# The last head's second V pair in one load, and wo in loads of 24, 6, 1 and 1 rows

## The chip, the cores and the metric

The kernel runs on one core of a Trainium2 chip. The metric is device time in microseconds (us) for one execution; the value for the kernel before is the median of three runs. Beside the runs there is one profiled execution. Its trace covers a span from the first to the last instruction, which is a little shorter than the execution's time. A position such as 358.86 is a number of microseconds from the start of that span.

## The reference

One token passes through two branches, and a gate mixes them. Branch A is attention over a long cache with grouped heads; branch B is a small gated MLP.

```python
# A: x (1,1,1024), k_cache and v_cache (1,4,65536,128), wq (1024,4096), wo (4096,1024), all bf16
q = (x @ wq) as 32 heads of 128
k, v = each of the 4 cached heads repeated for 8 query heads
p = softmax((q . k) * 128 ** -0.5)
a = (p @ v, the 32 heads side by side) @ wo
# B: w_in (1024,3584), w_out (1792,1024)
z = gelu(x @ w_in); z1, z2 = halves of z; z2 = layernorm(z2)
b = (z1 * (w_sp * z2 + b_sp)) @ w_out
# mix
g = sigmoid(sum(x * gate_w))
out = g * a + (1 - g) * b
```

The K and V caches are 67 MB each, so nearly everything that the kernel moves is cache: 162 MB are read in all, and each byte is used once.

## The kernel before

**Tiles.** A cached head has 65,536 rows of 128 values. It is cut into four tiles, 4 MB each, numbered j = 0 to 3 (`NT` = 4). In a tile each of the 128 partitions holds 128 rows (32 KB). Tiles come in pairs from one stretch of 256 rows per partition, so a load of two tiles reads 64 KB of each partition in one piece. All loads go into one SBUF buffer, `kv`, of five slots of 32 KB per partition (`NKV` = 5). `load(src, shape, at)` (L177) issues one DMA from SP into the slots from `at` on, and `load_kv` (L189) loads n tiles of one head from tile j on and returns the views. Reads and writes of the same slots order each other: a load waits until the last reader of what was there is done.

**The stages.** First come w_in and wq, the small branch's first half and the queries (L197 to L384). Then for each cached head g: four times `k_tile` (L407), which transposes the tile on DVE and multiplies it with the queries on PE; `stats(g)` (L431), the maximum, the exponentials on ACT and their transposes on DVE; four times `v_tile` (L457), 32 matmuls on PE for each tile, with 64 columns of weights each and 512 streamed columns, that accumulate into `o_ps`; and `head_out(g)` (L472). The loop at L529 interleaves the K tiles of head g with the V tiles of head g - 1. The last head's V tiles follow after the loop (L549 to L551).

**`head_out(g)`** takes the diagonal blocks of `o_ps` on DVE (L474), sums them into `o_sb` (L478), sends that and the sums of the exponentials through two small PE matmuls into `om_ps` (L482, L484), and ends with five short DVE instructions, the last of which writes the normalised and gated head into `oa` (L496).

**The projection.** `wo_view` gives each partition its 32 rows of wo, 2 KB each. The loop at L559 loads them in the pieces of `WO_SPLIT`, from slot 3 on, so that the first piece needs slot 3 free, which the last head's second V tile used. After each load `project` (L511) multiplies its rows with `oa`: four matmuls a row, of 256 streamed columns each, in four column groups of PE that run side by side. All of it accumulates into `out_ps`, in which `uT @ w_out` of branch B already stands. ACT then casts `out_ps` (L566), and two small DMAs from the queues of ACT and SP store it (L569).

**Filler matmuls.** `keep_busy(n)` (L499) issues n matmuls of 128x128 weights and 512 streamed columns on PE, whose results nobody reads. They are the instructions with `busy_ps` in the profile. In the kernel before, six stand ahead of the last `head_out`, sixteen after it, and `WO_BUSY` gives how many follow each piece of wo: none after the 24 rows, two after the 4 rows, one after the 2 rows, none after the single rows.

**Order.** The block at L572 to L579 makes each engine keep the order of the program as written. PE therefore meets V tiles, fillers, `head_out`'s matmuls and projection exactly in the order of the code, and SP issues the loads in theirs. Repeated weight loads of one operand are dropped (`same_weights`).

Of the kernel before, what the change touches and what calls it, by code (L numbers as in the profile page):

```python
# [21 lines left out]
CC = CT // VC  # L22
ZN = 448
HN = 512
WO_SPLIT = (24, 4, 2, 1, 1)
WO_BUSY = {24: 0, 4: 2, 2: 1, 1: 0}


@with_exitstack
def kernel(  # L30
# [18 lines left out]
    _, G, S, DH = A_k_cache.shape  # L49
# [15 lines left out]
    assert S % (P * CT) == 0 and F == 2 * NB * ZN and ZN == B * FC and HD == NHB * NB * HN  # L65
    assert NHB * NB == 2 * G and CC * B == 2 * HN and sum(WO_SPLIT) == OC

# [12 lines left out]
    def same_weights(ins):  # L80
        held.add(ins.ins.name)
# [95 lines left out]
    def load(src, shape, at):  # L177
        n = 1
        for s in shape:
            n *= s  # L180
        v = kv[:, int(at * CT * P):int(at * CT * P) + n]
        if len(shape) == 2:
            v = v.rearrange("p (a b) -> p a b", b=shape[1])
        ins = nc.sync.dma_start(out=v, in_=src)  # L184
        if not first_load:
            first_load.append(ins.ins.name)
        return v

    def load_kv(src, g, j, at, n=1):  # L189
        h, i = divmod(j, 2)  # L190
        rows = src[0, g, 2 * h * CT * P:2 * (h + 1) * CT * P, :].rearrange(
            "(p c) d -> p (c d)", c=2 * CT)
        v = load(rows[:, i * CT * DH:(i + n) * CT * DH], (n * CT * DH,), at)
        return [v[:, i * CT * DH:(i + 1) * CT * DH] for i in range(n)]
# [166 lines left out]
    for k in range(NHB):  # L361
# [3 lines left out]
                                                                   j=B, e=2),  # L365
# [91 lines left out]
    def v_tile(g, j, vt):  # L457
        if j == 0:
            o_ps[g] = pso.tile([P, 2, VC * DH], FP32, name="o_ps")
        vx = vt.rearrange("p (v c d) -> p c v d", v=VC, d=DH)  # L460
        for u in range(CC // 2):
            hs = slice(u % 2 * P // 2, (u % 2 + 1) * P // 2)
            for e in range(2):
                ins = nc.tensor.matmul(  # L464
                    o_ps[g][hs, e, :],
                    lhsT=ptt[g, j][:, 2 * u:2 * u + 2, :].rearrange("p c x -> p (c x)"),
                    rhs=vx[:, 2 * u + e], start=(j == 0 and u < 2),
                    stop=(j == NT - 1 and u >= CC // 2 - 2), skip_group_check=True)
                if e > 0:
                    same_weights(ins)  # L470

    def head_out(g):  # L472
        gs = slice(g * B, (g + 1) * B)
        nc.vector.tensor_tensor(  # L474
            out=om8, in0=o_ps[g][:].rearrange("p e (v d) -> p (e v) d", d=DH),
            in1=own_8[:].unsqueeze(2).to_broadcast([P, 2 * VC, DH]), op=ALU.mult)
        o_sb = wk.tile([P, DH], FP32, name="o_sb")
        nc.vector.tensor_reduce(out=o_sb[:], in_=om8.rearrange("p x d -> p d x"), axis=AX.X,  # L478
                                op=ALU.add)
        om_ps = psm.tile([P, DH + NT], FP32, name="om_ps", tag="m")  # L480
        hs = hsel[:].rearrange("p h q -> p (h q)")
        nc.tensor.matmul(om_ps[gs, DH:], lhsT=hs, rhs=lss[g][:], start=True, stop=True,  # L482
                         skip_group_check=True)
        nc.tensor.matmul(om_ps[gs, :DH], lhsT=hs, rhs=o_sb[:], start=True, stop=True,  # L484
                         skip_group_check=True)
        rl = wk.tile([P, 2], FP32, name="rl")
        nc.vector.reduce_sum(out=rl[gs, 0:1], in_=om_ps[gs, DH:], axis=AX.X)
        nc.vector.reciprocal(out=rl[gs, 1:2], in_=rl[gs, 0:1])
        om = wk.tile([P, QD, OC], FP32, name="om")
        nc.vector.tensor_tensor(  # L490
            out=om[gs], in0=om_ps[gs, :DH].rearrange("p (q c) -> p q c", c=OC),
            in1=own_q[gs, :].unsqueeze(2).to_broadcast([B, QD, OC]), op=ALU.mult)
        osum = wk.tile([P, OC], FP32, name="osum")
        nc.vector.tensor_reduce(out=osum[gs, :], in_=om[gs].rearrange("p q c -> p c q"),
                                axis=AX.X, op=ALU.add)
        nc.vector.tensor_scalar(out=oa[gs, :], in0=osum[gs, :], scalar1=rl[gs, 1:2],  # L496
                                scalar2=gate[gs, :], op0=ALU.mult, op1=ALU.mult)

    def keep_busy(n):  # L499
        ps = pss.tile([P, 2 * HN], FP32, name="busy_ps", tag="s")  # L500
        w = wt[G % 2][:].rearrange("p v b t u h -> p (v b t u h)")
        for i in range(n):
            ins = nc.tensor.matmul(ps[:, :HN], lhsT=w[:, :P], rhs=w[:, :HN], start=True,  # L503
                                   stop=True, skip_group_check=True)
            if i > 0:
                same_weights(ins)
# [4 lines left out]
    def project(w, n, vec, c0, first=False, last=False):  # L511
        for c in range(n):
            for t in range(NB):
                nc.tensor.matmul(  # L514
                    out_ps[t * B:(t + 1) * B, :],
                    lhsT=vec[:, c0 + c:c0 + c + 1].to_broadcast([P, B]),
                    rhs=w[:, c, t * NO:(t + 1) * NO],
                    start=(first and c == 0), stop=(last and c == n - 1),
                    skip_group_check=True)
# [9 lines left out]
    for g in range(1, G):  # L529
# [16 lines left out]
            if h == 0 and g + 1 < G:  # L546
                build_w(g + 1)
        head_out(g - 1)
    for j, n, at in ((0, 2, 2), (2, 1, 1), (3, 1, 0)):  # L549
        for i, vt in enumerate(load_kv(A_v_cache, G - 1, j, at, n)):  # L550
            v_tile(G - 1, j + i, vt)  # L551
    keep_busy(6)
    head_out(G - 1)
    keep_busy(16)


    wo_view = A_wo.rearrange("(p c) n -> p c n", c=OC)
    c0 = 0
    for n in WO_SPLIT:  # L559
        t = load(wo_view[:, c0:c0 + n, :], (n, D), 3 + c0 * D / (CT * P))  # L560
        project(t, n, oa, c0, last=(c0 + n == OC))
        keep_busy(WO_BUSY[n])
        c0 += n
# [46 lines left out]
```

## Time and profile before

| | |
|---|---|
| median of 3 runs | 381.88 us (381.71 to 381.96) |
| the profiled execution's own time | 381.88 us |
| its span | 380.5 us |
| mean granted TensorE clock | 0.839 |
| PE busy | 226.4 us (60%) |
| DVE busy | 211.2 us (56%) |
| ACT busy | 39.6 us (10%) |
| read from HBM | 162.01 MB, 426 GB/s over the span |
| share of the SP queue's packets in 16 DMA engines' span | 98.8% |

The page of the profile has these parts. A table of 40 slices of equal length gives for each engine the busy share in tenths (9 is 90% or more); the row PEclk is the clock that PE was granted, in tenths of full speed, and the row DMA is the mean busy share of the core's 16 DMA engines. The chain of waits follows the work back from the last instruction to what released it; each line has a start, a length and what it was. A timeline line has a start, a length, the engine, the line of the kernel (L464 is line 464), the operation, what it writes and reads, shapes, a count, and in brackets how long the engine had been idle and what ended that. In windows, each line is a stretch with its length, PE's busy time with the number of matmuls, the mean granted clock, the DMA share and GB/s. A matmul's end in the trace is modelled[...], so the last one of a row of matmuls looks longer than the spacing between them.

### The profile page before, as it was taken

The numbers are of one execution on the slowest core, as the hardware profiler recorded it, in microseconds if no ns is written. First come the engines' busy times: TensorE is split into PE (matmuls) and PEld (weight loads), VectorE is DVE, ScalarE is ACT, GpSimd is POOL, SyncE is SP. The second block draws the span as 40 slices with busy tenths as digits, with TensorE's granted clock in tenths as the row PEclk, the third lists the DMA queues.
The fourth block names the chain that finished last, engine by engine and source line by source line (L and its number), as shares of the span: only waits on it lengthen the run. The fifth ranks groups of instructions, "written<-read, shape, count | busy, mean of one in ns | idle before, by whom it ended". The sixth has DMA issues, their size and how long they took to land.

```text
span 380.5 us, 2602 instructions
## 1 busy us (share of the span) xinstructions
PE 226.4 (60%) x1397; PEld 55.6 (15%) x800; DVE 211.2 (56%) x207; ACT 39.6 (10%) x55; POOL 4.4 (1%) x10
## 2 busy tenths in 40 slices
PE   0060605967655784794499139762993197739386
PEld 0010101211211210121022001110220011202113
DVE  4134217989374947867893058678940397650040
ACT  1001000111104310114011001140110010500000
POOL 4000000000000000000000000000000000000000
PEclk9995765999958796999599758995898599959789
DMA  9999999999999999999999999999999999999995
GB/s 386 476 420 413 401 442 441 441 472 410 407 422 441 441 443 434 434 434 441 441 429 441 434 441 420 422 413 442 434 434 429 427 434 442 436 410 434 431 432 224
DMA packets 3655, 162.17 MB, mean 426 GB/s; under 512 B 440, under 2 KB 444, under 8 KB 828
## 3 DMA queue, kind: packets, MB, share of 16 engines
q1 hardware_dynamic: 3604, 162.01, 98.8%
q8 instruction: 8, 0.13, 0.1%
q14 instruction: 3, 0.02, 0.0%
q10 hardware_dynamic: 40, 0.01, 0.0%
HBM read 162.01 MB, written 0.00 MB: 426 GB/s over the span
## 4 chain that ended last, share of the span: by engine, by line
DMA 71%; PE 17%; DVE 9%; issue 2%; SPq 0%; ACTq 0%; ACT 0%; DVEq 0%
DMA kv<-in_A_k_cache_dram 52%; PE s_ps L419 13%; DVE kv L412 8%; DMA kv<-in_A_wo_dram 7%; DMA kv<-in_A_v_cache_dram 7%; DMA wb<-in_B_b_sp_dram 5%; PE o_ps L464 2%; PE z_ps L296 1%; SPq L184 0%; DVE mx L402 0%; ACTq L198 0%; PE small_ps L271 0%; ACT out_sb L566 0%; PE out_ps L514 0%; ACTq L199 0%
## 5 line engine op out<-in xcount | busy, mean ns | idle before, releaser
L419 PE MATMUL s_ps<-kv,wt 128*128 128x512 bf16 x512 | 132.8, 414 | 81.4 <-DVE kv L412 81.3
L412 DVE STREAM_TRANSPOSE kv<-kv 128x2048 int32<-128x2048 int32 x64 | 142.4, 2280 | 69.7 <-DMA kv<-in_A_k_cache_dram 69.7
L464 PE MATMUL o_ps<-kv,pt 128*64 128x512 bf16 x512 | 63.6, 408 | 14.3 <-DMA kv<-in_A_v_cache_dram 14.3
L419 PEld LDWEIGHTS <-wt 128*128 128x128 bf16 x256 | 26.4, 103 | 189.2 <-issue 117.9
L428 ACT CAST sc<-s_ps 128x1024 bf16<-128x1024 f32 x16 | 16.2, 1013 | 250.7 <-PE s_ps L419 250.7
L464 PEld LDWEIGHTS <-pt 128*64 128x64 bf16 x256 | 16.9, 117 | 57.9 <-issue 48.6
L454 DVE STREAM_TRANSPOSE pt<-sc 128x1024 bf16<-128x1024 bf16 x16 | 18.6, 1217 | 6.8 <-ACT sc L451 6.8
L474 DVE TENSOR_TENSOR rowt<-o_ps,own 128x1024 f32<-128x1024 f32 x4 | 4.8, 1195 | 26.5 <-PE o_ps L464 26.5
L451 ACT ACTIVATE sc<-sc,nb 128x1024 bf16<-128x1024 bf16 x16 | 18.2, 1137 | 12.2 <-DVE nb L447 12.2
L484 PE MATMUL om_ps<-o_sb,hsel 128*32 128x128 f32 x8 | 2.3, 388 | 18.3 <-DVE o_sb L478 18.3
L402 DVE TENSOR_TENSOR mx<-mx,sc 128x1024 bf16<-128x1024 bf16 x8 | 5.5, 687 | 13.6 <-ACT sc L428 13.6
L296 PE MATMUL q_ps<-kv,xT 128*32 128x512 bf16 x64 | 5.7, 534 | 7.2 <-DMA kv<-in_A_wq_dram 7.2
L252 PE MATMUL xb_ps<-xg,spread 8*128 8x256 bf16 x1 | 0.4, 364 | 13.5 <-DMA xg<-in_gate_w_dram 13.5
L478 DVE TENSOR_REDUCE o_sb<-rowt 128x128 f32<-128x1024 f32 x4 | 7.5, 1872 | 0.1
L363 DVE TENSOR_TENSOR rowt<-q_ps,own_b 128x512 f32<-128x512 f32 x2 | 1.3, 686 | 10.8 <-PE q_ps L296 10.8
L503 PE MATMUL busy_ps<-wt 128*128 128x512 bf16 x25 | 6.1, 381 | 0.0
L296 PE MATMUL z_ps<-kv,xT 128*32 128x448 bf16 x64 | 6.1, 572 | 0.0
L566 ACT CAST out_sb<-out_ps 128x256 bf16<-128x256 f32 x1 | 0.4, 372 | 46.4 <-PE out_ps L514 46.4
L256 DVE TENSOR_TENSOR xm<-xb_ps,sel_i 128x128 f32<-128x128 f32 x2 | 0.5, 286 | 8.2 <-PE xb_ps L252 8.2
L514 PE MATMUL out_ps<-kv,oa 128*32 128x256 bf16 x128 | 4.2, 273 | 1.4 <-DMA kv<-in_A_wo_dram 1.4
L435 DVE TENSOR_REDUCE m<-mx 128x1 f32<-128x1024 bf16 x4 | 4.8, 1209 | 0.1
L296 PEld LDWEIGHTS <-xT 128*32 128x32 bf16 x64 | 2.6, 137 | 14.7 <-issue 14.6
(90 smaller groups left out, 61.2 us busy)
## 6 DMA issues: line engine op xcount, KB each, us to landing
kv<-in_A_v_cache_dram SPq DMA_DIRECT2D x2, 4096.0 KB, 22.8
kv<-in_B_w_in_dram SPq DMA_DIRECT2D x1, 7168.0 KB, 19.7
kv<-in_A_wo_dram SPq DMA_DIRECT2D x1, 6144.0 KB
kv<-in_B_w_out_dram SPq DMA_DIRECT2D x1, 3584.0 KB
kv<-in_A_wo_dram SPq DMA_DIRECT2D x1, 1024.0 KB, 26.8
kv<-in_A_wo_dram SPq DMA_DIRECT2D x1, 512.0 KB
kv<-in_A_wo_dram SPq DMA_DIRECT2D x2, 256.0 KB
kv<-in_A_k_cache_dram SPq DMA_DIRECT2D x8, 27.6
```

The lines of the kernel that those rows point to most:

```text
L296: ins = nc.tensor.matmul(ps[t * B:(t + 1) * B, k * HN:k * HN + n], lhsT=xT[:, i * KH + c:i * KH + c + 1].to_broadcast([P, B]), rhs=w[:, c, ...
L402: nc.vector.tensor_tensor(out=mx[:], in0=mxs[g][:], in1=sc[:], op=ALU.max)
L412: nc.vector.transpose(out=kb[:, v * n:(v + 1) * n], in_=kb[:, v * n:(v + 1) * n])
L419: ins = nc.tensor.matmul(s_ps[:, k * HN:(k + 1) * HN], lhsT=wt[g % 2][:, v, b].rearrange("p a v h -> p (a v h)"), rhs=kx[:, b // 2, b % 2, ...
L428: nc.scalar.copy(out=sct[g, j][:], in_=s_ps[:])
L435: nc.vector.reduce_max(out=m1[:], in_=mxs[g][:], axis=AX.X)
L451: nc.scalar.activation(out=sct[g, j][:], in_=sct[g, j][:], func=ACT.Exp, scale=SCALE, bias=nb[:, 0:1], accum_out=lss[g][:, j:j + 1])
L454: nc.vector.transpose(out=ptt[g, j][:].rearrange("p c x -> p (c x)"), in_=sct[g, j][:])
L464: ins = nc.tensor.matmul(o_ps[g][hs, e, :], lhsT=ptt[g, j][:, 2 * u:2 * u + 2, :].rearrange("p c x -> p (c x)"), rhs=vx[:, 2 * u + e], sta ...
L474: nc.vector.tensor_tensor(out=om8, in0=o_ps[g][:].rearrange("p e (v d) -> p (e v) d", d=DH), in1=own_8[:].unsqueeze(2).to_broadcast([P, 2 ...
L478: nc.vector.tensor_reduce(out=o_sb[:], in_=om8.rearrange("p x d -> p d x"), axis=AX.X, op=ALU.add)
L503: ins = nc.tensor.matmul(ps[:, :HN], lhsT=w[:, :P], rhs=w[:, :HN], start=True, stop=True, skip_group_check=True)
```

## The change

Two things are changed in how data comes in at the end, and the fillers with them.

- The last head's V tiles came in three loads: tiles 0 and 1 into slots 2 and 3, tile 2 into slot 1, tile 3 into slot 0. Afterwards they come in two: tiles 0 and 1 into slots 2 and 3, tiles 2 and 3 in one load into slots 0 and 1.
- wo came in pieces of 24, 4, 2, 1 and 1 rows of each partition; afterwards of 24, 6, 1 and 1.
- Fillers: 40 are added after the first pair of V tiles; six after the second pair remain; those after the last `head_out` go from 16 to 4; two now follow the 24 rows of wo, and none the later pieces, where there were two after the 4 rows and one after the 2 rows.

```diff
-WO_SPLIT = (24, 4, 2, 1, 1)
-WO_BUSY = {24: 0, 4: 2, 2: 1, 1: 0}
+WO_SPLIT = (24, 6, 1, 1)
+WO_BUSY = {24: 2, 6: 0, 1: 0}
...
         head_out(g - 1)
-    for j, n, at in ((0, 2, 2), (2, 1, 1), (3, 1, 0)):
-        for i, vt in enumerate(load_kv(A_v_cache, G - 1, j, at, n)):
+    for j, at in ((0, 2), (2, 0)):
+        for i, vt in enumerate(load_kv(A_v_cache, G - 1, j, at, 2)):
             v_tile(G - 1, j + i, vt)
-    keep_busy(6)
+        keep_busy((40, 6)[j // 2])
     head_out(G - 1)
-    keep_busy(16)
+    keep_busy(4)
 
 
     wo_view = A_wo.rearrange("(p c) n -> p c n", c=OC)
```

## The prediction

> **What bounds the kernel now.** I read the 40-slice table first, then the chain of waits over the last 40 us, then PE's and DVE's timelines there, and last PE in windows. The slice table:
>
> ```profile
> PEclk9995765999958796999599758995898599959789
> DMA  9999999999999999999999999999999999999995
> ```
>
> The DMA engines are full in every slice but the last, so time is lost or won only by moving the last landing, or by work behind it. The chain of waits names that landing:
>
> ```profile
> 348.65 0.02 issue
> ...
> 350.46 27.89 DMA kv<-in_A_wo_dram
> 378.35 0.04 issue
> 378.39 0.32 PE out_ps L514 x4
> 378.71 0.02 issue
> 378.73 0.37 ACT out_sb L566
> ```
>
> The last wo row lands at 378.35; four matmuls, one cast and the store follow, to the span's end at 380.5. PE's timeline (start, length) shows the slack elsewhere:
>
> ```profile
> 339.43 9.20 PE L464 MATMUL o_ps<-kv,pt 128*64 128x512 bf16 x64 [2.11 <-DMA kv<-in_A_v_cache_dram]
> 349.14 3.65 PE L464 MATMUL o_ps<-kv,pt 128*64 128x512 bf16 x32 [0.52 <-DMA kv<-in_A_v_cache_dram]
> 358.86 6.26 PE L464 MATMUL o_ps<-kv,pt 128*64 128x512 bf16 x32 [6.08 <-DMA kv<-in_A_v_cache_dram]
> 365.05 1.47 PE L503 MATMUL busy_ps<-wt 128*128 128x512 bf16 x6
> ...
> 368.68 3.63 PE L503 MATMUL busy_ps<-wt 128*128 128x512 bf16 x16
> 373.41 3.24 PE L514 MATMUL out_ps<-kv,oa 128*32 128x256 bf16 x112 [1.10 <-DMA kv<-in_A_wo_dram]
> ```
>
> The fourth V tile took 6.26 us against 3.65 for the same work on the third: after 6.08 us of idling it ran at half clock. DVE finished oa at 370.09 (369.79 + 0.30), 3.3 us before the 24 rows of wo landed. So o_ps may be 3 us late without moving the end, but a slow projection may not. Last, PE in windows (length, busy us, clock, DMA share, GB/s):
>
> ```profile
> 77.49:80.90 3.41, 1.42 (x7) 1.00 0.96 412
> 80.90:84.31 3.41, 2.33 (x10) 1.00 1.09 471
> 118.45:121.86 3.41, 1.14 (x7) 1.00 1.20 519
> 121.86:125.27 3.41, 0.00 (x0) 0.50 0.84 365
> 330.06:333.47 3.41, 1.07 (x12) 1.00 0.87 370
> 333.47:336.89 3.42, 0.21 (x1) 0.50 1.02 441
> ```
>
> All 22 changes of clock from 29.7 to 364.2 us lie on one grid of 3.413 us. At full clock, a grid window with 1.42 us busy (0.42) keeps the clock; one with 1.14 or 1.07 (0.33, 0.31) loses it at its end. At half clock, a window 0.82 busy restores it and one 0.73 busy doesn't.
>
> [...]
>
> **The change part by part**, against the profiled execution (span 380.5, time 381.88, which is also the runs' median; 1.38 lies outside the span).
>
> *One V load for two.* Both old loads were issued together at 331.0, once the last reader of slot 1 was done (PE, 330.98). The merged load waits for that same reader; slot 0 was free earlier. SP issues one instruction fewer (0.33 to 0.43 us), 8 us before the queue runs dry, for nothing. The first pair landed at 339.38; the singles at about 349.12 and 358.84, so 9.74 + 9.72 = 19.46 us. Pairs before it landed 38.7 us per two loads (145.44, 184.14, 222.87 in the chain), 19.36 each. Gain 0.10 us.
>
> *wo in four loads.* All are still issued when the second V tile is done (348.65), 10 us before the queue runs dry, so one fewer issue of 0.42 us is hidden. 24 rows took 373.40 - 358.84 = 14.55 us, 0.606 a row; the last 8 took 378.35 - 373.40 = 4.95 against 4.85 at that rate, an excess of 0.10 over four loads, so a quarter of it, 0.03 us, goes. Both edits: -0.13 us, between 0 (the cost is the bytes') and -0.21 (all excess goes). The first landings stay near 373.4, the six rows' at 373.4 + 6 x 0.61 = 377.05, the last at about 378.2.
>
> *The third tile's 32 matmuls move behind the pair's landing.* The 40 fillers stand between. Sixteen took 3.63 us, or 0.216 each with 0.17 at the end; 40 take 8.64 + 0.17, from 348.66 to 357.5. That is 1.3 us before the pair lands, so they delay nothing, and a window holding that gap is at least 0.6 busy, so the clock stays full. A full-clock V matmul is (3.65 - 0.2) / 32 = 0.108 us; 64 take 6.9 + 0.2 = 7.1, from 358.8 to 365.9. Before, o_ps was done at 365.12: +0.8 us. If they started at half clock for two whole windows (6.83 us, 32 matmuls), they would take 10.5 us, to 369.3: oa near 374.2, under 1 us behind the landing. I take full clock.
>
> *oa.* DVE began 0.04 after o_ps and finished oa 4.93 later; so oa comes at about 370.9, still 2.5 us before wo. Cost on the path: nothing. Without that cover it is the 0.8 us.
>
> *Fillers after head_out, 16 to 4.* 12 x 0.216 = 2.6 us less PE work. PE now runs six fillers to 367.3, the om_ps matmuls at 369.1 to 369.5 (they wait for DVE's o_sb, +0.8), four fillers to about 370.45, then nothing until 373.4: 3.0 us idle where it was 1.1. Nothing waits for fillers; the price is the clock, below.
>
> *Fillers among wo.* Two after the 24 rows, none later: 2 x 0.216 + 0.17 = 0.6 us. A projection matmul at full clock is (3.24 - 0.22) / 112 = 0.027. So 24 rows (96) from 373.4 to 376.2 with tail, fillers to 376.7, 0.35 before the six rows land. Their 24 matmuls take 0.65, from 377.05 to 377.7; the first single row has landed by then (0.11), and PE waits for the last at 378.2. In all PE is some 0.75 us ahead of the landings.
>
> *Sum.* -0.13 and four hidden terms: span 380.4, time 380.4 + 1.38 = 381.8.
>
> **The rivals.** All hang on the windows between 367.4 and 373.4, where PE has 1.3 us of work in 6.0.
>
> *The clock falls late.* With the grid of this profile, the window 371.0 to 374.4 holds only 373.4 to 374.4, 0.30 busy: below 0.33, so half clock from 374.43 to 377.85. By then 38 matmuls are done; 58 at 0.054 (estimate: double) end at 377.55, the fillers at 378.15, six rows at 378.8, the last two at 379.0 + 0.2: 0.5 us over 378.7, time 382.4. With the fall at 372.6 it is half clock to 376.0: 48 slow, 48 fast matmuls to 377.3, fillers 377.7, rows 378.4 and 378.6 + 0.2, so +0.1. Windows beginning from 369.2 to 371.1 do this: over half of the grid's positions, a third of them with +0.3 or more.
>
> *The clock falls early, and the end is slower.* A window that begins between 367.4 and 369.1 holds the om_ps matmuls and four fillers: 1.3 of 3.41, 0.38. The trace kept the clock at 0.42 and lost it at 0.33; 0.38 lies between. If the bound is above it, the clock falls at 370.9 to 372.5, the next window is too idle to restore it, and the projection runs at half clock till 374.3 to 379. With this profile's grid (371.0 to 377.85): (377.85 - 373.4) / 0.054 = 83 slow matmuls, 13 fast to 378.2, fillers 378.65, rows 379.3 and 379.5 + 0.2: 1.0 over, time 382.9; over the grid 382.2 to 383.7. This decides from a fall before about 373.4 that isn't undone by 377. For it: 16 fillers became four in that very stretch. Against it: the two windows that fell hold many matmuls of a few columns[...].
>
> *The transfers save more.* [...] It needs 0.76 us of gain; at most 0.21 is in the rows above. *The fillers overrun or the pair starts cold*: the clock is full from 343.7 on, so 40 fillers could only overrun if it fell; at half clock they would end at 365.7 and cost up to 7 us on PE.
>
> **How the numbers follow.** Nothing exposed, 0.41 (381.8, own range 381.6 to 382.0); late fall, 0.22 (382.0 to 382.5); early fall, 0.32 (382.9), three quarters of it beyond +0.76; overrun or cold pair, 0.03; transfers, 0.02. About 0.2% (0.76 us) is what this measurement tells from no change. Same: 0.41 + 0.22 + 0.08 - 0.02 for other surprises = 0.69; slower 0.24 + 0.03 + 0.01 = 0.28; faster 0.03. The range goes from the transfers' full excess (381.67, so 381.6) to 383.2, which leaves out the top quarter of the early fall, the overrun and the fast case: about 0.13.
>
> **What would show it.** Right: one V landing near 358.8, forty fillers ending near 357.5, 64 V matmuls in 7.1 us, oa near 370.9, 24 rows' matmuls from 373.4 in 2.8 us at clock 1.00, and PE waiting for the last row. Wrong: a clock of 0.50 in the windows from 371 to 378 and the last matmuls ended by PE rather than the landing; or V matmuls still running at 369.

## The result and the profile after

The changed kernel takes 383.18 us (median of 6 executions, 382.25 to 383.73) against 381.87 for the kernel before (6 executions, 381.68 to 381.96). The ratio is 1.0032, 95% interval 1.0017 to 1.0046: slower, by 1.3 us between the medians. (The ratios in this document agree with the means of the executions, not with the medians.) The forecast had been 381.8, no change. The spans tell the same: 380.8 to 382.0 us after, where those of before, in all later comparisons with it, are 380.1 to 381.0 with a median of 380.4.

The profiled execution is one of the milder ones: span 381.0, time 382.43. PE's timeline at its end (start, length, then the instruction, count, and what ended the idle time before it; a few records are missing, so 40, six and two fillers show as 39, five and one):

```profile
348.02 8.81 PE L503 MATMUL busy_ps<-wt 128*128 128x512 bf16 x39
358.68 7.10 PE L464 MATMUL o_ps<-kv,pt 128*64 128x512 bf16 x64 [1.85 <-DMA kv<-in_A_v_cache_dram]
365.71 1.47 PE L503 MATMUL busy_ps<-wt 128*128 128x512 bf16 x5
...
369.34 1.04 PE L503 MATMUL busy_ps<-wt 128*128 128x512 bf16 x4
373.22 4.47 PE L514 MATMUL out_ps<-kv,oa 128*32 128x256 bf16 x96 [2.85 <-DMA kv<-in_A_wo_dram]
377.62 0.39 PE L503 MATMUL busy_ps<-wt 128*128 128x512 bf16 x1
378.16 1.06 PE L514 MATMUL out_ps<-kv,oa 128*32 128x256 bf16 x32
```

Down to the fillers at 369.34 the end runs as worked out, except that the 40 fillers are done at 356.83 and not at 357.5. The projection doesn't: 96 matmuls take 4.47 us, where 112 took 3.24 before, and the last 32 (six, one and one rows) then run in one piece with no wait for a landing between them. PE is behind the DMAs. The clock's changes in this trace lie on a grid of 3.413 us again. PE's windows, cut along that grid (length, PE's busy us, clock, DMA share, GB/s), show why:

```profile
356.40:359.81 3.41, 1.56 (x14) 1.00 0.90 389
359.81:363.22 3.41, 3.41 (x35) 1.00 1.00 432
363.22:366.64 3.42, 3.37 (x28) 1.00 0.87 374
366.64:370.05 3.41, 1.74 (x11) 1.00 1.03 437
370.05:373.46 3.41, 0.56 (x14) 1.00 0.88 375
373.46:376.88 3.42, 3.42 (x76) 0.50 0.83 337
376.88:380.29 3.41, 2.19 (x61) 1.00 0.05 18
```

The window from 370.05 to 373.46 holds 0.56 us of work, and at its end, 0.24 us after the projection began, the clock goes to half for one whole window. This is the sign of being wrong that the prediction named. The chain of waits ends accordingly:

```profile
348.13 25.05 DMA kv<-in_A_wo_dram
373.18 0.04 issue
373.22 4.47 PE out_ps L514 x96
377.69 0.32 PE busy_ps L503
378.01 0.15 issue
378.16 1.09 PE out_ps L514 x32
```

Before, the chain stayed with the DMA until the last row at 378.35. Now it leaves it at the 24 rows' landing at 373.18, and the remaining 6 us to the last matmul's end are PE's. The last matmul ends at 379.24, against 378.71.

### The profile page after: what moved, and what is told of

It reads as the page before. It is cut to its first block, busy times and chain, and to the rows that moved or that the text cites. A ratio compares the mean times of both kernels' runs of the same rounds, so it can differ in the third digit from the quotient of the medians.

```text
span 381.0 us, 2623 instructions
## 1 busy us (share of the span) xinstructions
PE 229.5 (60%) x1421; PEld 56.2 (15%) x800; DVE 211.2 (55%) x207; ACT 39.6 (10%) x55; POOL 4.4 (1%) x10
## 4 chain that ended last, share of the span: by engine, by line
DMA 70%; PE 20%; DVE 8%; issue 1%; ACTq 0%; ACT 0%; DVEq 0%
DMA kv<-in_A_k_cache_dram 52%; PE s_ps L419 15%; DVE kv L412 8%; DMA kv<-in_A_v_cache_dram 7%; DMA kv<-in_A_wo_dram 7%; DMA wb<-in_B_b_sp_dram 5%; PE o_ps L464 2%; PE out_ps L514 1%; PE z_ps L296 1%; PE small_ps L271 0%; ACTq L198 0%; ACT out_sb L566 0%; PE busy_ps L503 0%; ACTq L199 0%; ACTq L201 0%
## 5 line engine op out<-in xcount | busy, mean ns | idle before, releaser
L464 PE MATMUL o_ps<-kv,pt 128*64 128x512 bf16 x512 | 61.6, 400 | 9.3 <-DMA kv<-in_A_v_cache_dram 9.3
L503 PE MATMUL busy_ps<-wt 128*128 128x512 bf16 x49 | 11.6, 380 | 0.1
L514 PE MATMUL out_ps<-kv,oa 128*32 128x256 bf16 x128 | 5.5, 347 | 3.0 <-DMA kv<-in_A_wo_dram 2.8
L514 PEld LDWEIGHTS <-oa 128*32 128x32 bf16 x128 | 4.8, 123 | 4.4 <-issue 2.8
```

The lines of the kernel that those rows point to most:

```text
L464: ins = nc.tensor.matmul(o_ps[g][hs, e, :], lhsT=ptt[g, j][:, 2 * u:2 * u + 2, :].rearrange("p c x -> p (c x)"), rhs=vx[:, 2 * u + e], sta ...
L514: nc.tensor.matmul(out_ps[t * B:(t + 1) * B, :], lhsT=vec[:, c0 + c:c0 + c + 1].to_broadcast([P, B]), rhs=w[:, c, t * NO:(t + 1) * NO], st ...
```

## The experiments

**Which part costs.** Four kernels, with the fillers after the last `head_out` as the dose. The first puts the 16 back into the changed kernel:

```diff
     head_out(G - 1)
-    keep_busy(4)
+    keep_busy(16)
```

> The changed kernel with the 16 fillers after the last head_out put back (4 to 16), all else as changed. Theory (the clock falls in the hole that the cut of these fillers leaves before the wo rows land): the fillers reach from 369.3 to 372.9, no window of 3.41 us is less than half busy, the projection runs at full clock, and the time is 381.75 us, a little below the kernel before. Rival W (the split of wo, its six-row piece or the fillers moved among wo): still 383.2. Rival V (the third and fourth V tiles start later and push oa): still 383.2.

Measured: 381.70 us against 381.77, ratio to before 1.0005 (0.9997 to 1.0013). The spans are 379.9 to 380.6; three of 13 executions spend 2.1 to 2.7 us outside the span, where 1.4 to 1.5 is usual (more on this below). Rivals W and V fall: with both of their edits in place and only this number undone, the loss is gone. Its windows on the grid:

```profile
367.72:371.13 3.41, 2.13 (x11) 1.00 0.97 414
371.13:374.55 3.42, 3.17 (x61) 1.00 0.86 361
374.55:377.96 3.41, 2.94 (x86) 1.00 0.54 213
```

None of these windows is under 0.62 busy, and PE again waits for the last rows (its timeline):

```profile
373.21 2.80 PE L514 MATMUL out_ps<-kv,oa 128*32 128x256 bf16 x96 [0.24 <-DMA kv<-in_A_wo_dram]
375.94 0.60 PE L503 MATMUL busy_ps<-wt 128*128 128x512 bf16 x2
376.91 0.95 PE L514 MATMUL out_ps<-kv,oa 128*32 128x256 bf16 x28 [0.36 <-DMA kv<-in_A_wo_dram]
378.18 0.29 PE L514 MATMUL out_ps<-kv,oa 128*32 128x256 bf16 x4 [0.32 <-DMA kv<-in_A_wo_dram]
```

The other way round, the cut alone in the kernel before:

```diff
     head_out(G - 1)
-    keep_busy(16)
+    keep_busy(4)
```

> The kernel before with only the fillers after the last head_out cut from 16 to 4; loads, wo split and its fillers as before. Theory: the hole reaches from 369.6 to 373.4 (3.8 us, head_out being 0.8 us earlier than in the changed kernel), so this alone costs at least as much as the whole change: 383.0 to 383.7. Rivals W and V: 381.9, as before.

Measured, in five executions: 383.11 us, ratio 1.0040 (1.0027 to 1.0054), spans 381.3 to 382.6. One number makes a loss as large as the whole change's, without any of the loads changed. Its windows on the grid:

```profile
364.17:367.58 3.41, 2.54 (x18) 1.00 1.07 461
367.58:371.00 3.42, 1.38 (x6) 1.00 0.87 374
371.00:374.41 3.41, 0.90 (x20) 0.50 0.85 351
374.41:377.82 3.41, 3.41 (x72) 0.50 0.66 254
```

This is the prediction's early fall: a window with the `om_ps` matmuls and the four fillers, 1.38 us or 0.40 busy, loses the clock at 371.0; the next is too idle to bring it back; the projection runs at half clock until 377.8.

Eight fillers in the changed kernel, and in another kernel none (the same line with 0):

```diff
     head_out(G - 1)
-    keep_busy(4)
+    keep_busy(8)
```

> The changed kernel with 8 fillers after the last head_out in place of 4. Theory: the fillers end near 371.2, the hole before 373.3 is 2.1 us instead of 3, and a window is poor in work for fewer positions of the clock's grid; time between 381.8 and 382.7. Rivals W and V: 383.2, the same as with 4.

Measured: 381.88 us, ratio 1.0009 (1.0000 to 1.0018); four of 13 spans are 380.8 to 380.9, the others 380.0 to 380.3. The profiled one is of the four; there the clock fell after a window with 1.44 us, 0.42 busy. PE's longest pause in it, the one before the projection in its timeline, was 1.97 us, far shorter than a window:

```profile
366.56:369.98 3.42, 1.75 (x11) 1.00 1.03 436
369.98:373.39 3.41, 1.44 (x21) 1.00 0.91 386
373.39:376.80 3.41, 3.41 (x76) 0.50 0.84 339
```

```profile
369.16 1.90 PE L503 MATMUL busy_ps<-wt 128*128 128x512 bf16 x8
373.02 4.47 PE L514 MATMUL out_ps<-kv,oa 128*32 128x256 bf16 x96 [1.97 <-DMA kv<-in_A_wo_dram]
```

The kernel with none:

> The changed kernel with no filler after the last head_out. Theory: the hole is 3.9 us with almost no work before it, the clock falls early for nearly every position of its grid, and the time is 383.3 to 383.8, above that with 4. Rivals W and V: 383.2 or a little less, since nothing else depends on these fillers.

Measured: 382.90 us, ratio 1.0032 (1.0020 to 1.0043), spans 380.9 to 382.0. A miss, and a useful one: no filler costs no more than four. Its windows:

```profile
367.65:371.06 3.41, 0.41 (x2) 1.00 0.93 396
371.06:374.48 3.42, 1.39 (x28) 0.50 0.83 352
374.48:377.89 3.41, 3.41 (x72) 0.50 0.58 226
```

I had supposed that four fillers save the clock at some positions of the grid where none would lose it. They don't: in the kernel before with the cut, a window that holds all four is 0.40 busy and the clock falls as it does with none. What a fall then costs is left to where the grid lies against the projection; that is argued, since each kernel has one trace.

**Where the bound lies.** All ten traces up to here and in the next group, read along their own grids, give it for these kernels. They are counted from the first change of clock on, at 29.7 us in the trace of the kernel before, which ahead of it shows 1.00 even in windows without any PE work. At full clock, every window up to 0.416 busy lost it, 27 of them with 0.28 or more; of seven between 0.417 and 0.426, five kept it; above 0.43 all kept it but two at 0.46 and 0.48, both of which hold the small fp32 matmuls of `stats` (the 0.46 is 1.57 of 3.41 us, from 117.45 in the trace of the changed kernel). Two of the falls near the bound, at 0.412 and 0.419, come after windows with `s_ps` matmuls of 512 columns alone, so small matmuls aren't needed for them. The first, from the kernel with the 40 fillers alone (in the next group), with the start of the window that follows:

```profile
159.49:162.91 3.42, 1.41 (x8) 1.00 1.33 575
162.91:164.00 1.09, 1.09 (x4) 0.50 0.14 60
```

At half clock, none up to 0.752 got it back, and all from 0.772 on did; of three between, one did. (The two windows of the trace of before that the prediction puts at 0.73 and 0.82 are 2.44 and 2.76 us, 0.71 and 0.81.) The prediction let the grid lie anywhere against the start of the span; its position does differ between the ten traces, by up to 1.7 of its 3.41 us.

Laid over the timeline of the changed kernel, the bound of these traces leaves no safe position. As an estimate from that timeline: a window of 3.41 us that begins anywhere from 367.3 to 371.2 holds at most 1.42 us of work. That stretch is 3.9 us long, longer than a window, so wherever the grid lies, one of its windows begins there. With eight fillers the poorest windows hold 3.41 - 1.97 = 1.44 us, right at the bound, which fits four long spans of 13.

**The other parts alone.** wo's split with its fillers:

```diff
-WO_SPLIT = (24, 4, 2, 1, 1)
-WO_BUSY = {24: 0, 4: 2, 2: 1, 1: 0}
+WO_SPLIT = (24, 6, 1, 1)
+WO_BUSY = {24: 2, 6: 0, 1: 0}
```

> The kernel before with only wo's split and its fillers changed (24, 6, 1 and 1 rows, two fillers after the 24). Theory of the hole: no hole, so the clock stays and the span is as before or up to 0.05 us less, time 381.75. Rival W (the coarser split or the moved fillers cost): above 382.3. On the excess outside the span that some executions of the changed kernel show (time minus span over 2 us): none here, if the merged load or the longer PE program brings it.

Measured: 381.85 us, ratio 0.9999 (0.9991 to 1.0007). Nothing, either way.

The merged V load with the 40 fillers:

```diff
-    for j, n, at in ((0, 2, 2), (2, 1, 1), (3, 1, 0)):
-        for i, vt in enumerate(load_kv(A_v_cache, G - 1, j, at, n)):
+    for j, at in ((0, 2), (2, 0)):
+        for i, vt in enumerate(load_kv(A_v_cache, G - 1, j, at, 2)):
             v_tile(G - 1, j + i, vt)
-    keep_busy(6)
+        keep_busy((40, 6)[j // 2])
```

> The kernel before with only the merged V load and the 40 fillers behind the first pair; 16 fillers after head_out and wo in five loads as before. Theory of the hole: no hole, 0.10 to 0.15 us off the span, median 381.7. Rival V (the third tile's work behind the pair's landing pushes the end): above 382.3. Excess outside the span in some executions, if the merged load or the longer PE program brings it.

Measured: 381.96 us, ratio 1.0010 (1.0003 to 1.0017), a small loss where a small gain was expected. Two things make it. Fourteen of 21 spans are 380.2 to 380.5, seven are 380.9 to 381.3. And four executions spent 2.1 to 3.0 us outside the span, where 1.4 to 1.5 is usual (one of them has both). What lengthened the seven no trace shows.

The 40 fillers alone, with the loads as before:

```diff
         for i, vt in enumerate(load_kv(A_v_cache, G - 1, j, at, n)):
             v_tile(G - 1, j + i, vt)
+        if j == 0:
+            keep_busy(40)
```

> The kernel before with the 40 fillers after the second V tile and nothing else: three V loads, 16 fillers after head_out, wo in five. The third tile's matmuls wait for the fillers until 357.5 and end at 361, the fourth's, now at full clock, at 364.9, so oa is as before: span 380.4, time 381.9. Tells apart what brings the excess outside the span: if the longer PE program does, some of these executions have it (time minus span over 2 us); if the merged load does, none.

Measured: 381.94 us, ratio 1.0008 (1.0000 to 1.0016). One of 13 executions has 2.59 us outside the span, so the merged load isn't needed for it. Two spans are 381.3 and 381.4. Here the third and fourth tiles' 64 matmuls take 7.10 us, both at full clock, oa comes earlier and the 16 fillers end at 371.66, 1.77 us before the wo rows; an execution with more room still could lose the clock there. No trace shows it.

The merged load without its 40 fillers, 16 after `head_out`:

```diff
-        keep_busy((40, 6)[j // 2])
+        keep_busy((0, 6)[j // 2])
     head_out(G - 1)
-    keep_busy(4)
+    keep_busy(16)
```

> The changed kernel with 16 fillers after head_out, but without the 40 fillers behind the first V pair. PE idles for 10 us before the pair lands, so the 64 V matmuls begin at half clock: 8.5 to 10.2 us in place of 7.1, the 16 fillers then end at 374.4 to 376.1, after the wo rows have landed, and the projection starts behind them. Theory of the clock: 0.2 to 1.7 us over the same kernel with the 40 fillers, time 381.9 to 383.4, nearest 382.6. If the clock didn't matter for the pair: 381.7.

Measured: 382.56 us, ratio 1.0019 (1.0010 to 1.0028), spans 380.3 to 381.7. Its timeline, of an execution whose span is the shortest of these:

```profile
358.64 8.45 PE L464 MATMUL o_ps<-kv,pt 128*64 128x512 bf16 x64 [9.76 <-DMA kv<-in_A_v_cache_dram]
367.03 1.47 PE L503 MATMUL busy_ps<-wt 128*128 128x512 bf16 x6
...
370.65 3.63 PE L503 MATMUL busy_ps<-wt 128*128 128x512 bf16 x16
374.21 2.80 PE L514 MATMUL out_ps<-kv,oa 128*32 128x256 bf16 x96
```

The pair takes 8.45 us in place of 7.10, the clock being half until 361.4, and the projection no longer waits for wo but stands behind the 16 fillers, a microsecond after the rows are there. Here that still fits before the end; that the longer executions begin the pair at half clock for longer is argued, since none was traced. With 16 fillers after `head_out`, those ahead of the pair are needed, and those behind it can be in the way.

**The two leftovers.** Were the long spans of the kernel with the merged load, 40 and 16 fillers clock falls as well? The end of the 40 goes with the time at which the first pair got its full clock: 343.7 in the trace of before, where the pair was done at 348.65, and 342.7 in that of the changed kernel, where it was done at 348.11 and the 40 at 356.83, which leaves 1.85 us to the second pair's landing. One more change narrows that hole:

```diff
-        keep_busy((40, 6)[j // 2])
+        keep_busy((44, 6)[j // 2])
     head_out(G - 1)
-    keep_busy(4)
+    keep_busy(16)
```

> The changed kernel with 44 fillers in place of 40 behind the first V pair and 16 in place of 4 after head_out, so that both holes on PE are short: the fillers end between 357.4 and 359.1, wherever the clock's grid lies, and the pair lands near 358.7. Theory: in the kernels with 40 and 16 the spans of 380.9 to 381.4 come from executions in which the first pair ran early at full clock, the fillers ended near 356.8, and a grid window with under 0.42 of work ended before the pair landed. Here no window is so poor: every span between 379.9 and 380.6, median time 381.7. If those spans have another cause, one execution in four or five has a span of 380.9 or more here too. The excess outside the span may still appear.

Measured: 381.87 us, ratio 0.9999 (0.9990 to 1.0007). All 13 spans are 380.2 to 380.5, and the hole before the pair is 0.28 us. But this doesn't show that the four more fillers removed the long spans. They were seen with wo in five loads; the kernel with 40 and 16 fillers that has wo in four, the first of these experiments, differs from this one by the four fillers alone and had no span above 380.6 either, in 13. So wo's split may be what matters, or chance; no run here separates them. Its timeline:

```profile
348.95 9.67 PE L503 MATMUL busy_ps<-wt 128*128 128x512 bf16 x44
358.91 7.10 PE L464 MATMUL o_ps<-kv,pt 128*64 128x512 bf16 x64 [0.28 <-DMA kv<-in_A_v_cache_dram]
```

And the time outside the span:

```diff
     build_w(0)
+    keep_busy(40)
     for j, at in ((0, 2), (2, 0)):
         for i, kn in enumerate(load_kv(A_k_cache, 0, j, at, 2)):
```

> The kernel before with 40 fillers near 50 us, ahead of the first K tile, where PE waits for K's landing and transposes; the end of the kernel is as before. Tells what brings the excess outside the span (over 2 us for a few executions of each kernel with 40 more fillers): if the longer PE program does, 1 to 4 of some 13 executions have it here as well; if the fillers near the end do, none. Span 380.4, median 381.8 to 381.9 in both cases.

Measured: 381.89 us, ratio 1.0004 (0.9996 to 1.0012), all 13 spans 380.2 to 380.6; two executions spend 2.51 and 2.90 us outside the span. So 40 more matmuls seem to bring it some 300 us from the end as well. In all, 15 of 98 executions of kernels with the 40 or 44 fillers show over 2 us outside the span, none of the 30 of the three without them, and none of the 99 of the kernel before in these comparisons. What happens there stays open: the trace ends with the span.

## Why the prediction was wrong

**What held.** The merged load landed at 358.68 (worked out: near 358.8); the 40 fillers were done 1.85 us before it and delayed nothing; the third tile's matmuls waited for that landing with the fourth's, and the 64 took 7.10 us (7.1); oa came at 370.74 (370.9); the four fillers ended at 370.38 (370.45). Neither the third tile's late work nor oa was on the path, nor was wo's split (the kernel with it alone: 0.9999). The transfers' gain of 0.13 us seems to be there too. All landings together lie up to 0.3 us earlier or later from one trace to another, so it has to be read from the first V pair's first matmul to the last wo row's: three traces with the loads of before (that of the kernel before, and those with 40 fillers added late or early) give 38.96, 38.96 and 39.03 us; the two with both loads changed in which PE waits for that row (16 fillers after `head_out`, 40 or 44 before) give 38.86 and 38.84. It is too small for the time to show.

**What failed** is the last step on the fillers after `head_out`, and with it the choice among the rivals. The price of the 12 missing fillers was put down as "the clock, below", the right place; then the bound for keeping the clock was left anywhere between 0.33 and 0.42, and I took it to be below the 0.38 of the window with four fillers, with the argument that the two windows which fell held small matmuls. They hold three of seven and two of twelve, and that these made a difference was not shown. In the ten traces the bound is 0.42, at the top of that interval. With it, the main line, in which nothing is exposed, was open at no position of the grid, and it had been given the best chance, 0.41. The early fall, put at 0.32, is what the cut does in the kernel with the cut alone, where the window of 0.40 falls, and four fillers cost about as much as none. The changed kernel's own trace shows the late fall, put at 0.22 though the prediction's working gave it over half of the grid's positions even with a low bound; that the longer executions fell early is argued from the other two kernels. The trace of before had no window between 0.34 and 0.419 and couldn't decide it; the argument for a lower bound was a guess, and it was given more weight than the plain fact that a quarter of the fillers was left in a stretch of two windows. Windows of 512-column matmuls alone fell at 0.412 and 0.419 as well, and the window with the four fillers itself holds small fp32 matmuls, those of `om_ps`.

**The sizes.** The early fall was priced at 382.2 to 383.7, 382.9 for one position of the grid. Measured are 382.25 to 383.73, median 383.18, above the 382.9; of this, one execution's 383.73 is a span of 381.3 with 2.43 us outside it, which the prediction had no term for. Without that excess (at 1.45) it would be 382.75 and the median 382.87. The profiled execution is a late fall, at 373.46: with 9 fast matmuls, 63 slow ones at 0.054 and 24 fast, the prediction's rates give 0.25 + 3.41 + 0.65 + 0.2 = 4.5 us, and 4.47 was measured. The rate of the projection at half clock, an estimate, was right. For an early fall at 371.0 the prediction had 1.0 us over; the kernel with no filler, where the clock fell at 371.06, has a span of 381.5, 1.0 above the 380.5 of the kernel before. A gap that was not priced is the 0.15 us between the last filler and the six rows. One figure in the early fall's working doesn't follow: a fall at 370.9 that the next window can't undo lasts to 377.7 at least on the measured grid (370.9 + 2 x 3.413), not to 374.3, and in both traces of an early fall half clock ends at 377.8 or 377.9.

**A second hole.** That a window holding the gap between the 40 fillers and the pair "is at least 0.6 busy" was worked out from one end of the first pair, 348.66. Where the grid lies otherwise the pair is done by 348.0, the gap grows to 1.85 us, and the window around it in the changed kernel's trace is 1.56 us or 0.46 busy, just above the bound. Falls there would fit the longer spans of the kernel with the merged load and 40 fillers alone, but no trace of such an execution was taken, and the kernel with wo in four loads besides had none of them; their cause stays open.

## What to carry to other kernels

Treat filler work as a part of the critical path's price even where nothing waits for it: here 4 fillers in place of 16 took the kernel before from 381.77 to 383.11 us. Before taking it away, cut the trace into the windows on which its clock changes (3.413 us here), see how full the poorest one gets, and price the work that follows it at half clock (here 4.47 us for 96 matmuls, most of them at half clock, in place of 2.80). Where the cover must hold for any position of that grid, which differed by up to 1.7 us between these traces, ask it of every stretch as long as a window, not of the one in the trace. And when a bound is known only as an interval and the case falls inside it, price the worse end unless the trace decides.

## What the runs showed of the hardware

A window needn't be idle to cost PE its clock, and a pause needn't be as long as a window. In ten traces of these kernels, from the first change of clock on, it fell after every window busy for up to 0.416 of 3.41 us. Of seven windows between 0.417 and 0.426 it fell after two, one of which (1.44 us, in the kernel with eight fillers) held no pause longer than 1.97 us. From 0.43 on it was kept, except after two windows with small fp32 matmuls (0.46 and 0.48). It came back after every window of 0.772 or more, and after none up to 0.752. With 40 or 44 more matmuls in PE's program, near its start or near its end, 15 of 98 executions spent 2.1 to 3.0 us outside the span, where 1.4 to 1.5 is usual; none of 129 without them did. Why is open.
